# Loading w2 by two transfers (112 and 16 partitions) instead of one of 128

## The chip, the cores and the metric

The kernel runs on one core of a Trainium2 chip. The metric is the device time of one execution in microseconds (us), here the median of several runs.

## What is computed

One decode step with two branches for B = 2 tokens of width 448. Branch A is attention over the last W = 2048 positions of a key and value cache, branch B a small feed-forward net. Their product is added to the input. All inputs are bf16.

```python
xn = layernorm(x)                                  # x: 2 x 1 x 448
q = (xn @ wq).reshape(2, 1, 16, 256)               # wq: 448 x 4096
k, v = last 2048 positions of the caches           # 2 x 8 heads x 2048 x 256, each head serves 2 q heads
s = softmax(q k^T * 256**-0.5) v  -> 2 x 1 x 4096, @ wo        # wo: 4096 x 448
g = silu(relu(xn @ w1) @ w2)                       # w1: 448 x 1792, w2: 1792 x 448
out = x + s * g
```

## The kernel before

A program class, `_Prog`, keeps one list of operations for each engine. `pr.op` appends an instruction and `pr.dma` (line 34) a transfer to the list of the engine that issues it; both take a list of earlier operations to wait for. `run` turns the waits into semaphore waits: each transfer has a semaphore of its own, and each list is issued in its order. Since all operations go through this helper, all transfers carry line 35 and all matmuls line 241 in the profile, and tiles tell them apart.

**Transfers.** All large loads are issued by SP, in one queue: wq, w1, w2, then the four K tiles (`kv[0]` to `kv[3]`, 4 MB each, one for a batch and four of the eight heads), then V into the same four buffers, and last wo in six pieces (`WO_PARTS`). The first seven have nothing to wait for. V of unit u (`load_v`) waits for the last score matmul of unit u, because it overwrites K; V of unit 3 is loaded in two halves. wo overwrites wq's buffer and waits for the q matmuls. ACT's queue carries only the small loads of x and half of the output.

**w2** has 1792 x 448 elements. `w2_src` views it as 128 rows of 14 x 448 elements: partition p holds the 14 rows 14p to 14p + 13 of the matrix in one run of 12,544 bytes. `w1_sb` and `w2_sb` both appear as `w_sb` in the profile, because numbers are left out of names there.

**Order of the work.** DVE computes the layer norm; PE transposes xn and multiplies it with wq when that has landed; q is spread into a stationary form (`qstat`). Then come `do_H` (w1, relu, a transpose into `h_sb`) and `do_F`: 14 matmuls of `h_sb` with `w2_sb`, a sum over column groups, and the silu on ACT and DVE. `do_F` waits for w2, for h and for a cleared bank. After it, for each unit u, `do_turn` transposes the K tile in four pieces on DVE (line 276), `do_S` computes the scores on PE, and `do_max` and `do_et` the maximum, the exponential and its transpose. When all four units are through, `do_PV` multiplies with V unit by unit, `do_out` scales, and `do_turn_out` brings the result into the form for wo. The matmuls with wo follow as its pieces land, and two DVE instructions (lines 474 and 476) form the output. `fill` issues matmuls whose result nobody reads.

Of the kernel before, what the change touches and what calls it, by code (L numbers as in the profile page):

```python
# [11 lines left out]
PE, DVE, ACTE, SP, POOL = "pe", "dve", "act", "sp", "pool"  # L12
# [62 lines left out]
def bass_recurrent_scan__sliding_block_cached__dense_activation_relu__decode_kernel(  # L75
# [32 lines left out]
    with es:  # L108
        pr = _Prog(nc, es)

        def named(name, shape, dt):
            return es.enter_context(nc.sbuf_tensor(name, shape, dt))

        def psum(name, shape, dt):
            return es.enter_context(nc.psum_tensor(name, shape, dt))
# [48 lines left out]
        w2_sb = named("w2_sb", [128, 14 * D], BF)  # L164
# [8 lines left out]
        fbk = psum("fbk", [128, 512], F32)  # L173
# [10 lines left out]
        w2_src = B_w2.rearrange("(p j) n -> p (j n)", j=14)  # L184
# [3 lines left out]
        st = {}  # L188
        d_wq = pr.dma(SP, wqo[:, 0:SLOTS * HC], wq_src)
        st["w1"] = pr.dma(SP, w1_sb[:, :], w1_src)  # L190
        st["w2"] = pr.dma(SP, w2_sb[:, :], w2_src)
        for u in range(NU):
            d_k[u] = pr.dma(SP, kv[u][:, :], kv_src(u, A_k_cache))

# [16 lines left out]
        def z(t):  # L211
            return a_z[t.name]
# [27 lines left out]
        def mm(out_ap, lhsT, rhs, start, stop=False, **kw):  # L240
            return lambda e: e.matmul(out_ap, lhsT=lhsT, rhs=rhs, start=start, stop=stop,  # L241
                                      skip_group_check=True, **kw)
# [9 lines left out]
        deps = [d_wq, v_xr, z(qbk)]  # L252
        for s in range(SLOTS):
            for i in range(4):
# [3 lines left out]
                deps = []  # L258
# [5 lines left out]
        deps = [v_qx, st["mbk"]]  # L264
        for n in range(16):
            m_qt = pr.op(PE, mm(mbk[:, 16 * n:16 * n + 16], q_x[:, 128 * n:128 * n + 128],
                                view(ident, 0, [[32, 4], [1, 4]]), n == 0), deps)
            deps = []
# [116 lines left out]
            st["h"] = pr.op(DVE, lambda e: e.transpose(h_sb[:, :], h_n[:, :]), [v])  # L385

        def do_F():
            deps = [st["w2"], st["h"], z(fbk)]
            for j in range(14):
                i = j % 4  # L390
                o = pr.op(PE, mm(fbk[32 * i:32 * i + B, 0:D], h_sb[:, 32 * j:32 * j + 2], w2_sb[:, j * D:j * D + D],
                                 j < 4, j >= 10, tile_position=(0, 32 * i)), deps)
                deps = []
            v = pr.op(DVE, lambda e: e.tensor_copy(zc[:, :], fbk[:, 0:D]), [o])
            deps = [v, v_f8, st["mbk"]]
            for c in range(2):
                o = pr.op(PE, mm(mbk[32 * c:32 * c + B, 0:NCOL], f8[:, 0:B], zc[:, NCOL * c:NCOL * c + NCOL],
                                 True, True, tile_position=(0, 32 * c)), deps)
                deps = []
            a_e = pr.op(ACTE, lambda e: e.activation(ea[0:ROWS, :], mbk[0:ROWS, 0:NCOL], ACT.Exp, scale=-1.0), [o])  # L400
            v = pr.op(DVE, lambda e: e.tensor_scalar(
                out=ea[0:ROWS, :], in0=ea[0:ROWS, :], scalar1=1.0, scalar2=None, op0=ALU.add), [a_e])
            v = pr.op(DVE, lambda e: e.reciprocal(tmp[0:ROWS, :], ea[0:ROWS, :]), [v])
            st["g"] = st["mbk"] = pr.op(DVE, lambda e: e.tensor_tensor(
                out=g_sb[0:ROWS, :], in0=mbk[0:ROWS, 0:NCOL], in1=tmp[0:ROWS, :], op=ALU.mult), [v])
# [3 lines left out]

        do_H()  # L410
        do_F()
        do_turn(0, 0, 4)
        do_S(0)
# [31 lines left out]
        deps = [st["at"], z(wbk)]  # L445
        for j in range(WO_TILED):
# [3 lines left out]
            deps = []  # L450
# [13 lines left out]
        deps = [v_wc]  # L464
        for c in range(2):
            pr.op(PE, mm(fbk[32 * c:32 * c + B, 0:NCOL], f8[:, 0:B], wc[:, NCOL * c:NCOL * c + NCOL], False,
                         tile_position=(0, 32 * c)), deps)
            deps = []
# [42 lines left out]
```

## Time and profile before

| What | Value |
|---|---|
| median of 3 runs | 110.72 us (110.68 to 110.85) |
| the profiled execution's own time | 110.67 us |
| its span, from the first to the last instruction | 109.3 us |
| busy: PE, DVE, ACT, POOL | 57.0, 62.2, 9.1, 2.1 us |
| read from HBM | 44.11 MB, 403 GB/s over the span |
| mean granted clock of TensorE | 0.842 |

The profile is a page of one execution, and a trace that answers questions on it. Times are us from the start of the span. PE is TensorE's matmul, PEld its weight load, DVE is VectorE, ACT is ScalarE, POOL is GpSimd, SP is SyncE, and SPq is SP's issue of transfers. L35 is line 35 of the kernel. The page cuts the span into 40 equal slices (2.73 us each) and gives the busy share of each in tenths; the line DMA is the mean busy share of the core's 16 DMA engines, and GB/s is what they moved. In lists of waits and in timelines, `<-` names what released an instruction after an idle time. The chain is the sequence of work that ended last, followed back from the last instruction.

### The profile page before, as it was taken

What the parts mean: (1) busy time and instruction counts of PE and PEld (TensorE: products, weight loads), DVE (VectorE), ACT (ScalarE), POOL (GpSimd) and SP (SyncE); (2) the same over time, 40 slices, a digit from 0 to 9 for tenths busy, and PEclk for the clock granted to TensorE, in tenths of its full rate; (3) what the DMA queues carried; (4) which work ended last, traced back from release to release, by engine and by line L of the source; (5) the groups of instructions that cost most, each with busy time, mean ns of one, the idle gap of its engine ahead of it and who ended that gap; (6) DMA issues with size and microseconds to landing.
All of it is one profiled execution on the core that took longest, in us unless ns stands there. A gap on an engine that the chain in (4) does not pass through costs nothing.

```text
span 109.3 us, 1081 instructions
## 1 busy us (share of the span) xinstructions
PE 57.0 (52%) x458; PEld 14.5 (13%) x458; DVE 62.2 (57%) x83; ACT 9.1 (8%) x18; POOL 2.1 (2%) x12
## 2 busy tenths in 40 slices
PE   0010559430000079929952994499339555937791
PEld 0000114100000011001100120010023122413230
DVE  2920046445099979999999999930457333004102
ACT  3970000010000000002000200020110000000000
POOL 7000000000000000000000000000000000000000
PEclk9999999985555555999995569958995999999999
DMA  6899999999999999999999999999999899999940
GB/s 168 336 452 397 408 436 501 396 455 438 444 396 455 467 408 396 455 467 408 408 458 444 408 420 467 432 420 402 467 432 420 378 444 420 444 413 410 405 187 1
DMA packets 2616, 44.17 MB, mean 404 GB/s; under 512 B 306, under 2 KB 564, under 8 KB 948
## 3 DMA queue, kind: packets, MB, share of 16 engines
q1 hardware_dynamic: 2596, 44.11, 94.7%
q8 instruction: 3, 0.05, 0.2%
q14 instruction: 1, 0.01, 0.0%
q10 hardware_dynamic: 16, 0.00, 0.0%
HBM read 44.11 MB, written 0.00 MB: 403 GB/s over the span
## 4 chain that ended last, share of the span: by engine, by line
DMA 57%; DVE 28%; PE 7%; SPq 5%; issue 1%
DMA kv<-in_A_k_cache_dram 34%; DVE kv L276 24%; DMA wqo<-in_A_wo_dram 23%; PE sbk L241 7%; SPq L35 5%; DVE q_x L305 1%; DVE rm L293 1%; DVE rm_t L295 0%; DVE bias L299 0%; DVE bt L296 0%; DVE tmp L474 0%; DVE out_sb L476 0%; PE fbk L241 0%
## 5 line engine op out<-in xcount | busy, mean ns | idle before, releaser
L241 PE MATMUL sbk<-kv,qstat 128*8 128x512 bf16 x128 | 29.9, 1086 | 23.9 <-DVE kv L276 23.9
L276 DVE STREAM_TRANSPOSE kv<-kv 128x2048 f32<-128x2048 f32 x16 | 35.6, 2276 | 4.6 <-DMA kv<-in_A_k_cache_dram 4.6
L241 PE MATMUL obk<-kv,pt 128*16 128x512 bf16 x128 | 9.3, 435 | 4.8 <-DVE xg L356 2.4
L241 PEld LDWEIGHTS sbk<-kv,qstat 128*8 128x8 bf16 x128 | 4.0, 107 | 48.4 <-DVE kv L276 30.2
L353 DVE TENSOR_SCALAR o_odd<-obk,rs 128x256 f32<-128x256 f32 x4 | 1.9, 484 | 11.6 <-PE obk L241 11.6
L300 ACT ACTIVATE e_sb<-sbk,bias 128x512 bf16<-128x512 f32 x4 | 2.7, 687 | 52.6 <-DVE bias L299 52.6
L241 PE MATMUL qbk<-wqo,xr 128*4 128x512 bf16 x28 | 3.2, 626 | 5.7 <-DMA wqo<-in_A_wq_dram 5.7
L259 DVE TENSOR_SCALAR q_x<-qbk 128x512 bf16<-128x512 f32 x1 | 0.7, 691 | 8.7 <-PE qbk L241 8.7
L293 DVE TENSOR_REDUCE rm<-sbk 128x1 f32<-128x512 f32 x4 | 2.6, 662 | 4.7 <-PE sbk L241 4.7
L241 PE MATMUL sbk<-kv,ident 128*32 128x512 bf16 x19 | 5.1, 380 | 0.0
L241 PEld LDWEIGHTS obk<-kv,pt 128*16 128x16 bf16 x128 | 3.2, 97 | 10.1 <-issue 5.8
L305 DVE STREAM_TRANSPOSE q_x<-e_sb 128x512 bf16<-128x512 bf16 x4 | 2.8, 691 | 1.7 <-ACT e_sb L300 1.7
L241 PE MATMUL mbk<-ident,xg 2*128 2x2 bf16 x7 | 0.3, 163 | 6.0 <-DVE xg L234 6.0
L322 DVE TENSOR_TENSOR pt<-spk,pmask 128x512 bf16<-128x512 f32 x4 | 2.6, 684 | 0.7 <-PE spk L241 0.7
L241 PE MATMUL qbk<-w_sb,xr 128*2 128x448 bf16 x28 | 2.8, 572 | 0.0
L241 PE MATMUL fbk<-wqo,at 128*2 128x224 bf16 x32 | 2.5, 258 | 0.4 <-DMA wqo<-in_A_wo_dram 0.4
L241 PE MATMUL spk<-q_x,perm 128*32 128x128 bf16 x16 | 0.6, 292 | 3.1 <-DVE q_x L305 3.1
L474 DVE TENSOR_TENSOR tmp<-fbk,g_sb 34x224 f32<-34x224 f32 x1 | 0.4, 383 | 3.1 <-PE fbk L241 3.1
L270 DVE CAST qstat<-mbk 32x256 bf16<-32x256 f32 x4 | 1.7, 421 | 0.7 <-PE mbk L241 0.7
L356 DVE SCALAR_TENSOR_TENSOR xg<-obk,rs,o_odd 128x256 bf16<-128x256 f32 x4 | 1.9, 484 | 0.1
L451 DVE COPY wc<-wbk 128x448 f32<-128x448 f32 x1 | 0.6, 625 | 2.4 <-PE wbk L241 2.4
L241 PEld LDWEIGHTS sbk<-kv,ident 128*32 128x32 bf16 x19 | 1.8, 97 | 1.8
(70 smaller groups left out, 33.1 us busy)
## 6 DMA issues: line engine op xcount, KB each, us to landing
kv<-in_A_k_cache_dram SPq DMA_DIRECT2D x4, 4096.0 KB, 41.3
kv<-in_A_v_cache_dram SPq DMA_DIRECT2D x3, 4096.0 KB, 22.1
kv<-in_A_v_cache_dram SPq DMA_DIRECT2D x2, 2048.0 KB, 18.0
wqo<-in_A_wq_dram SPq DMA_DIRECT2D x1, 3584.0 KB, 11.3
w_sb<-in_B_w_dram SPq DMA_DIRECT2D x2, 1568.0 KB, 16.2
wqo<-in_A_wo_dram SPq DMA_DIRECT2D x1, 1792.0 KB, 23.7
wqo<-in_A_wo_dram SPq DMA_DIRECT2D x3, 448.0 KB, 24.8
wqo<-in_A_wo_dram SPq DMA_DIRECT2D x2, 224.0 KB, 25.5
```

The lines of the kernel that those rows point to most:

```text
L35: o = _Op(eng, lambda e: e.dma_start(dst, src), [d for d in deps if d is not None], True)
L241: return lambda e: e.matmul(out_ap, lhsT=lhsT, rhs=rhs, start=start, stop=stop, skip_group_check=True, **kw)
L259: v_q = pr.op(DVE, lambda e: e.tensor_scalar(out=view(q_x, 0, [[256, 8], [128, 2], [1, 32]]), in0=view(qbk, 0, [[64, 8], [1, 2], [2, 32]]) ...
L270: st["q"] = st["mbk"] = pr.op(DVE, lambda e, Q=Q: e.tensor_copy(qstat[32 * Q:32 * Q + 32, 256 * Q:256 * Q + 256], mbk[32 * Q:32 * Q + 32, ...
L276: st["turn", u] = pr.op(DVE, lambda e, n=n: e.transpose(kf[:, 2048 * n:2048 * n + 2048], kf[:, 2048 * n:2048 * n + 2048]), [d_k[u]])
L293: v = pr.op(DVE, lambda e: e.tensor_reduce(out=rm[:, 0:1], in_=sbk[u % 2][:, :], axis=AX.X, op=ALU.max), [last_S[u], p_z, st.get(("rmt", u ...
L300: st["exp", u] = pr.op(ACTE, lambda e: e.activation(e_sb[:, :], sbk[u % 2][:, :], ACT.Exp, bias=bias[:, 0:1], accum_out=ssum[:, u:u + 1]), ...
L305: st["et", u] = pr.op(DVE, lambda e: e.transpose(q_x[:, 512 * u:512 * u + 512], e_sb[:, :]), [st["exp", u], m_qt])
L322: st["pt", u] = pr.op(DVE, lambda e: e.tensor_tensor(out=view(pt[u], 0, [[8, 64], [2, 4], [1, 2]]), in0=view(spk, 128 * u, [[2, 64], [0, 4 ...
L353: v = pr.op(DVE, lambda e: e.tensor_scalar(out=o_odd[:, :], in0=obk[:, DH:2 * DH], scalar1=rs[:, 2 * u + 1:2 * u + 2], scalar2=None, op0=A ...
L356: st["osb", u] = pr.op(DVE, lambda e: e.scalar_tensor_tensor(out=o_sb[:, lo:lo + DH], in0=obk[:, 0:DH], scalar=rs[:, 2 * u:2 * u + 1], in1 ...
L451: v_wc = pr.op(DVE, lambda e: e.tensor_copy(wc[:, :], wbk[:, 0:D]), [o])
```

## The change

The one transfer of w2 becomes two on the same queue, one after the other: rows 0 to 111 and rows 112 to 127. Each has its own semaphore, and `do_F` waits for both. The bytes, their places and everything else stay as they were.

```diff
         st["w1"] = pr.dma(SP, w1_sb[:, :], w1_src)
-        st["w2"] = pr.dma(SP, w2_sb[:, :], w2_src)
+        st["w2a"] = pr.dma(SP, w2_sb[0:112, :], w2_src[0:112, :])
+        st["w2"] = pr.dma(SP, w2_sb[112:128, :], w2_src[112:128, :])
         for u in range(NU):
             d_k[u] = pr.dma(SP, kv[u][:, :], kv_src(u, A_k_cache))
...
         def do_F():
-            deps = [st["w2"], st["h"], z(fbk)]
+            deps = [st["w2a"], st["w2"], st["h"], z(fbk)]
```

## The prediction, made before the changed kernel ran

> **What bounds the kernel now.** I read the page's 40 slices first, then the DMA queues, the chain, and busy time by stretches.
>
> ```profile
> DMA  6899999999999999999999999999999899999940
> GB/s 168 336 452 397 408 436 501 396 455 438 444 396 455 467 408 396 455 467 408 408 458 444 408 420 467 432 420 402 467 432 420 378 444 420 444 413 410 405 187 1
> ```
> ```profile
> q1 hardware_dynamic: 2596, 44.11, 94.7%
> q8 instruction: 3, 0.05, 0.2%
> ```
>
> From the third slice to the 38th the DMA engines are busy nine tenths or more. SP's one queue (q1) carries everything but the x loads and one half of the output. The stretches give the rate (columns: start:end, length, busy us and count of PE, PEld, DVE, ACT, POOL, then PE clock, DMA share, GB/s):
>
> ```profile
> 39.00:58.00 19.00, 14.95 (x64) 1.91 (x64) 18.18 (x13) 0.78 (x2) 0.00 (x0) 0.86 1.01 437
> 58.00:77.00 19.00, 14.55 (x64) 2.04 (x64) 13.72 (x15) 1.55 (x4) 0.00 (x0) 0.74 1.01 435
> ```
>
> 436 GB/s over 16 engines is 27.25 B/ns each. At that rate the 44.11 MB of q1 need 44,110 / 436 = 101.2 us of a 109.3 us span. The trace's packet records (start, size, duration; I give their times from the span's start) agree: data runs from 1.76 us to 106.48 us, each 12,544 B packet of w2 took 469 ns, each 32,768 B packet of K and V 1,213 ns, one after another on every engine. The chain's end:
>
> ```profile
> 81.24 25.50 DMA wqo<-in_A_wo_dram
> 106.75 0.04 issue
> 106.79 0.38 PE fbk L241 x4
> 107.19 0.40 DVE tmp L474
> 107.61 0.38 DVE out_sb L476
> ```
>
> The last piece of wo waits 25 us in the queue, lands, and 1.3 us of compute and the output follow. The DVE part of the chain (24% on the K transposes) looks like a second bound, but V is issued well ahead of need: V3 at 77.5 us, while the queue still had over 8 us of V2 to move. So the end is set by the queue: what makes w2 take longer moves everything behind it by the same amount, K, the transposes, V and wo alike.
>
> **The change part by part.** *Issue on SP.* One more instruction. SP issues back to back from 0.74 us; w1 and w2 took 0.41 and 0.46 us:
>
> ```profile
> 1.20 0.92 SPq L35 DMA_DIRECT2D w_sb<-in_B_w_dram  x2
> 2.16 2.74 SPq L35 DMA_DIRECT2D kv<-in_A_k_cache_dram  x4
> ```
>
> So the four K issues move from 2.16 to about 2.6 us. K0's data starts at about 18.3 us, behind wq, w1 and w2. The cover is 16 us; cost nothing. SP's next issue, V0 at 46.54, waits for PE, not for SP.
>
> *The added wait.* PE waits for both pieces before F; the pieces' landing is what matters. What stands there now:
>
> ```profile
> L35 SPq DMA_DIRECT2D w_sb<-in_B_w_dram x2: 408/435/462, 1.2 to 1.7; - x2
> DMA to landing us min/median/max: 14.5/16.2/17.8
> ```
> ```profile
> 20.63 0.65 DVE L385 STREAM_TRANSPOSE h_sb<-h_n 128x448 bf16<-128x448 bf16 x1
> 22.34 0.62 DVE L394 COPY zc<-fbk 128x448 f32<-128x448 f32 x1 [1.06 <-PE fbk L241]
> 25.88 0.38 DVE L404 TENSOR_TENSOR g_sb<-mbk,tmp 34x224 f32<-34x224 f32 x1
> 30.05 8.89 DVE L276 STREAM_TRANSPOSE kv<-kv 128x2048 f32<-128x2048 f32 x4 [3.79 <-DMA kv<-in_A_k_cache_dram]
> ```
>
> w2 was issued at 1.66 and landed at 1.66 + 17.8 = 19.5 us; F starts at 21.38, after h (20.63 + 0.65 = 21.28). The first 1.8 us of a later landing are hidden by h. Queued behind the wait on PE is S of unit 0, and behind F's results on DVE the first K transpose; both wait for K0 anyway, with 3.79 us of idle DVE, and K0 moves with w2. Cost nothing, even if w2 is 3.8 us late.
>
> *Semaphore packets.* Every 128-row transfer ends in 16 packets of 4 B, one per engine (18 such transfers and the 2-row output give the 288 + 2 that I count on q1), of 9 ns each. One more per engine: 0.01 us.
>
> *Where the rows go.* This is the term that matters. Bytes and row size stay the same. Before, each engine took 8 rows, and sixteen streams at once did not slow one another. After, each takes 7 of the 112 rows (16 divides 112) and one of the 16 rows. If the write side of a group of eight partitions takes no more than one engine's stream (a stream never showed more than 27.25 B/ns, to eight partitions), two engines that write into one group share its rate. The trace shows no large transfer that is not 128 partitions wide, so both ends must be worked out. Lower end: streams never disturb each other, 0.01 us. The nearest row for that is x_sb: two 896 B packets to partitions 0 and 1, 1 ns apart, took 39 ns each, what 896 / 27.25 = 33 ns and some 6 ns of overhead give for one alone; but they are 14 times shorter than a w2 row. A gain is excluded here, since no engine gets less to move. Upper end: the 112 rows fill 14 groups, so 8 x 0.469 = 3.75 us where engines would need 7 x 0.469 = 3.28: 0.47 more. The last 16 rows are two groups, with sixteen engines writing: again 8 x 0.469 = 3.75 us, where alone it is 0.47: 3.28 more. Together 3.75 us.
>
> I take half, 1.9 us. The large back-to-back w2 rows resemble the second piece more than the 39 ns packets do, so it is not zero; but the engines arrive spread out (w1's semaphore packets lie between 14.54 and 15.42, 0.88 us), so that sharing is partial, an engine that is through goes on to K0, and the groups of eight may lie so that fewer than eight meet.
>
> [...]
>
> *Sum.* The profiled execution took 110.67 us (span 109.3 and 1.4 around it), 0.05 under the median of 110.72. 110.67 + 0.01 + 1.9 = 112.6 us. Late next: K0 by 1.9 us, and through the queue wo's last piece, at 108.6 instead of 106.75.
>
> **The rivals.** *No disturbance at all (chance 0.18).* The write side has room, or each engine keeps the same partitions: 110.67 + 0.01 = 110.7 us, no change. For it: the 39 ns pair. Against it: 27.25 B/ns is the ceiling of every stream, and all large streams of this trace are one to eight partitions, so the trace has never tested it.
>
> *Rows dealt unevenly to engines (0.07).* If an engine always takes eight rows, 112 rows go to 14 engines and the 16 rows to 2 of the same. These two then hold 16 rows of w2 instead of 8, 8 x 0.469 = 3.75 us more, and they set the end: 114.4 us. Against it: the four 2-row transfers on ACT's queue leave eight semaphore packets, two each, so the count of engines follows the rows and is not fixed at eight rows each. [...]
>
> *Rows dealt in turn (0.06).* If row p of the 112 goes to engine p mod 16, neighbours meet in one group all the time, not only at the edges. With two sharing throughout, w2 takes twice 3.75 us, 114.4; with four, 15.0 us, 122. Against it: nothing in the trace tells the order; for 128 rows any such order would show streams under full rate, and none is.
>
> *Faster (0.07).* The engines do not end together: their last packets end between 104.47 and 106.48, three of them late (106.12, 106.28, 106.48), the next at 105.50. The late ones had an instruction load (q8, 16,384 B) between their K and V rows: a 32,768 B packet with one beside it took 1.68 us or more instead of 1.213, and a 16,384 B packet of V by itself takes 0.61. One more DMA and wait move the instruction stream. If the loads then fall on engines that are early, the end comes 0.20 us earlier (one load) to 0.98 us earlier (all three); with 0.4, 110.3 us. It decides only where the w2 rows cost less than that. Against it: one instruction among 1081 hardly moves a load of 16 KB.
>
> **How the numbers follow.** The forecast has the remaining 0.62. Slower by over 0.2% (0.22 us, about what a measurement of this kernel can tell from no change) are the forecast and the two deals of rows: 0.62 + 0.07 + 0.06 = 0.75. Within 0.2%: 0.18. Faster: 0.07. The range must take in the no-change case, since the other cases leave out more than 0.2 without it, and the upper bound of the sharing: 110.5 to 114.4, which leaves out the dearer deals and most of the gain. The forecast's own range is 111.2 (the 112 rows' 0.47 alone) to 114.4 (all 3.75).
>
> **What would show it.** Right: packets of 12,544 B that take well over 469 ns, in the last row of each engine most; w2's second piece landing some 1 to 3 us after 19.5; K0's first transpose near 32 instead of 30.05; the wait for F still short; the end of wo near 108.6. GB/s would dip in the slices between 15 and 22 us alone. Wrong: all 256 packets still at 469 ns, which makes it the no-change case; or engines with 16 packets and others with 8; or delays of K0 that are not there at wo, which would mean that the queue has slack that I have not seen.

## The result, and the profile after

The changed kernel takes 114.31 us (median of four runs, 113.50 to 114.38), the kernel before 110.70 us beside it: a ratio of 1.0308, 95% interval 1.0268 to 1.0348, so by the ratio some 3.4 us slower (the medians differ by 3.6). The profiled execution took 113.50 us with a span of 112.2 us, 2.83 us over the one shown of before; it is the fastest of the four. The forecast of 112.6 us had the direction and the cause, but was too low by about 1.7 us: the result lies at the very top of the range of 110.5 to 114.4. One execution of the two halves below (lower and upper) took 123.57 us, at a granted clock of 0.747 where its others had 0.819 to 0.954, and is left out of the times and ratios here.

The page of the changed kernel, its 40 slices:

```profile
DMA  6898999999899899899999999999999999999950
GB/s 164 348 461 382 429 349 282 239 491 426 374 467 456 386 444 479 386 432 467 409 424 456 421 432 432 444 409 450 444 397 456 403 403 432 444 419 397 408 207 1
```

The DMA line is as full as before, but for three slices (from 14 to 22.4 us) the same busy engines move 349, 282 and 239 GB/s. Before, the lowest of these three was 396. Everything behind runs at the old rate again. The same in stretches of 3 us:

```profile
12.00:15.00 3.00, 3.00 (x28) 0.77 (x28) 0.00 (x0) 0.00 (x0) 0.00 (x0) 1.00 0.99 422
15.00:18.00 3.00, 1.61 (x32) 0.88 (x32) 2.08 (x4) 0.00 (x0) 0.00 (x0) 1.00 1.04 293
18.00:21.00 3.00, 1.83 (x20) 0.41 (x12) 1.94 (x5) 0.00 (x0) 0.00 (x0) 1.00 1.36 328
```

Before, these stretches had 431, 427 and 504 GB/s. (A packet is counted where it starts, so a short stretch can exceed the real rate.) From 15 to 18 us the DMA share is 1.04 at 293 GB/s, where before it was 1.00 at 427: the engines are as busy and move less. The packet records say the same directly: w1's 128 packets of 12,544 B take 469 ns each as before. Of the 128 of w2 only 8 do; in order of start, sixteen at a time, the medians from the second sixteen on are 694, 724, 734, 688, 646, 734 and 903 ns, and the longest takes 1,255. The longer times do not end with w2's own packets: the first K0 packet of each engine takes 1,388 to 2,752 ns, where before all sixteen took 1,213. Over these full-rate lengths, w2's packets cost each engine 1.98 us and the first K0 packet 0.95 us in the mean, together 2.93, about the 2.83 that the execution is longer.

What this does further on, first w1 (1568 KB) and w2's two pieces (the issue list, with KB and us to landing), then PE at F, then DVE:

```profile
w_sb<-in_B_w_dram SPq DMA_DIRECT2D x1, 1568.0 KB, 15.1
w_sb<-in_B_w_dram SPq DMA_DIRECT2D x1, 1372.0 KB, 20.1
w_sb<-in_B_w_dram SPq DMA_DIRECT2D x1, 196.0 KB, 20.5
```
```profile
22.70 0.92 PE L242 MATMUL fbk<-w_sb,h_sb 128*2 128x448 bf16 x14 [2.86 <-DMA w_sb<-in_B_w_dram]
```
```profile
20.54 0.65 DVE L386 STREAM_TRANSPOSE h_sb<-h_n 128x448 bf16<-128x448 bf16 x1
27.56 0.38 DVE L405 TENSOR_TENSOR g_sb<-mbk,tmp 34x224 f32<-34x224 f32 x1
33.24 8.89 DVE L277 STREAM_TRANSPOSE kv<-kv 128x2048 f32<-128x2048 f32 x4 [5.29 <-DMA kv<-in_A_k_cache_dram]
42.91 2.32 DVE L277 STREAM_TRANSPOSE kv<-kv 128x2048 f32<-128x2048 f32 x1 [0.78 <-DMA kv<-in_A_k_cache_dram]
```

PE now waits 2.86 us for w2 and starts F at 22.70 instead of 21.38. Nothing that matters waits for it: DVE is through with F at 27.94 and idle for 5.29 us before K0. K0's transposes start 3.19 us later (33.24 for 30.05) and K1's too (42.91 for 39.72). The chain's end carries it to the output, wo's last landing at 109.57 instead of 106.75:

```profile
84.47 25.10 DMA wqo<-in_A_wo_dram
109.57 0.04 issue
109.62 0.38 PE fbk L242 x4
```

### The profile page after: what moved, and what is told of

Read it like the earlier page. It is cut to its first block, busy times and chain, and to the rows that moved or that the text cites. A ratio compares the mean times of both kernels' runs of the same rounds, so it can differ in the third digit from the quotient of the medians.

```text
span 112.2 us, 1083 instructions
## 1 busy us (share of the span) xinstructions
PE 57.5 (51%) x458; PEld 15.0 (13%) x458; DVE 62.2 (55%) x83; ACT 9.1 (8%) x18; POOL 2.1 (2%) x12
## 4 chain that ended last, share of the span: by engine, by line
DMA 58%; DVE 27%; PE 7%; SPq 5%; issue 1%
DMA kv<-in_A_k_cache_dram 35%; DVE kv L277 24%; DMA wqo<-in_A_wo_dram 22%; PE sbk L242 7%; SPq L35 5%; DVE q_x L306 1%; DVE rm L294 1%; DVE rm_t L296 0%; DVE bias L300 0%; DVE tmp L475 0%; DVE bt L297 0%; DVE out_sb L477 0%; PE fbk L242 0%
## 5 line engine op out<-in xcount | busy, mean ns | idle before, releaser
L242 PE MATMUL fbk<-w_sb,h_sb 128*2 128x448 bf16 x14 | 0.9, 351 | 2.9 <-DMA w_sb<-in_B_w_dram 2.9
```

## The experiments

"Sharing" is the theory of the prediction: engines that write into the same few partitions share one write path. Its rivals: a second transfer costs by itself (issue, semaphore, a gap in the queue), or the uneven or small pieces do. In the windows quoted below the last number is GB/s. These are the same windows of the kernel before:

```profile
15.00:19.00 4.00, 2.61 (x44) 1.20 (x44) 2.93 (x6) 0.00 (x0) 0.00 (x0) 1.00 1.13 485
19.00:23.00 4.00, 1.84 (x26) 0.41 (x18) 1.89 (x3) 0.00 (x0) 0.00 (x0) 1.00 0.95 410
```

**A second transfer without other partitions.**

```diff
-        st["w2"] = pr.dma(SP, w2_sb[:, :], w2_src)
+        st["w2a"] = pr.dma(SP, w2_sb[:, 0:12 * D], w2_src[:, 0:12 * D])
+        st["w2"] = pr.dma(SP, w2_sb[:, 12 * D:14 * D], w2_src[:, 12 * D:14 * D])
```

> w2 as two transfers of 128 partitions each, split by columns (12/14 and 2/14 of each row): the second transfer, its semaphore, issue and wait stay, the partition ranges go. Sharing theory (engines that write into the same few partitions share one write path): no cost but eight more packets and a semaphore packet per engine at some 8 to 9 ns each, +0.07 us, 110.8 us, all w2 packets at their full-rate length. Rival, the second transfer as such costs the time (its issue, semaphore or a gap in the queue): 113.5 to 114.4 us as in the changed kernel.

Measured: 110.75 us, ratio 1.0005 (0.9988 to 1.0023). The packets keep their full-rate lengths (10,752 B in 404 ns, 1,792 B in 74). The issue, the semaphore, the wait and the small second transfer cost nothing that can be measured. The rival falls.

**The 16-row piece by itself**, beside an untouched w2:

```diff
         st["w2"] = pr.dma(SP, w2_sb[:, :], w2_src)
+        st["w2x"] = pr.dma(SP, kv[3][112:128, 0:14 * D], w2_src[112:128, :])
...
-            d_k[u] = pr.dma(SP, kv[u][:, :], kv_src(u, A_k_cache))
+            d_k[u] = pr.dma(SP, kv[u][:, :], kv_src(u, A_k_cache), [st["w2x"]] if u == 3 else [])
...
-            deps = [st["w2"], st["h"], z(fbk)]
+            deps = [st["w2"], st["w2x"], st["h"], z(fbk)]
```

The issue of K3 now waits for the extra load. It is through by 21.9 us, while the queue still holds K0 to K2.

> The kernel before, with an extra load of w2's rows 112 to 127 into 16 partitions (112 to 127) of the K3 buffer, which K3 overwrites later; it measures the 16-row piece by itself. Its bytes at full rate are worth 0.47 us. Without sharing: 111.2 us. Sharing in groups of eight neighbouring partitions (two groups for 16 rows): 3.75 us for the piece, 114.4 us. [...] The rival that any second transfer costs about 3 us: 113.7 us or more, and the same in the run with spread partitions.

Measured: 112.68 us against 110.75, ratio 1.0179 (1.0146 to 1.0213): 1.93 us, about four times the 0.469 us of one packet (1.88), as if the sixteen rows lay in four groups of four that take one row at a time (an estimate from these two numbers). That is 1.46 us over its bytes. Twelve packets of 12,544 B that start between 18.5 and 19.5 us take 575 to 1,441 ns, the rest of them there 469, and each engine's first K0 packet takes 1,299 to 2,427.

```profile
19.00:23.00 4.00, 1.79 (x26) 0.35 (x18) 1.83 (x3) 0.00 (x0) 0.00 (x0) 1.00 0.93 339
```

Most of the dip lies between 19 and 21 us: 187 GB/s there, where the kernel before has 426.

**The 112-row piece by itself**, in the same way (`kv[3][0:112, 0:14 * D]` from `w2_src[0:112, :]`).

> The kernel before, with an extra load of w2's rows 0 to 111 into partitions 0 to 111 of the K3 buffer; it measures the 112-row piece by itself. Its bytes at full rate are worth 7 x 0.469 = 3.28 us, so 114.0 us without sharing. Sharing, with the groups of partitions as the limit: 8 x 0.469 = 3.75 us, 114.5 us. If most of the changed kernel's cost (2.8 us) comes from this piece, it is 116 us or more.

Measured: 116.30 us, ratio 1.0505 (1.0468 to 1.0541): 5.55 us, 2.27 over its bytes. That is over both figures worked out for it. The window shows it while this piece runs:

```profile
19.00:23.00 4.00, 0.00 (x0) 0.00 (x0) 0.99 (x2) 0.00 (x0) 0.00 (x0) 0.83 1.04 294
```

The two excesses, 1.46 and 2.27, make 3.73 us; the change itself costs 3.4 (2.97 to 3.85 by the interval's ends). So the sum of the pieces agrees with the cost, and the larger part is in the large piece.

**Sixteen rows spread out** (`kv[3][0:128:8, 0:14 * D]` from `w2_src[0:128:8, :]`, the rest as above).

> As the extra 16-row load, but into partitions 0, 8, 16 ... 120 (and from the same rows of w2), one row in each group of eight neighbours. Same bytes, same number of packets, other places. Sharing in groups of eight neighbours: each engine has a group of its own, 0.47 us, 111.2 us. [...] No sharing: 111.2 us, and then the run with neighbouring partitions is 111.2 us too.

Measured: 111.98 us, ratio 1.0111 (1.0076 to 1.0145): 1.23 us, 0.76 over its bytes and 0.70 less than with neighbouring partitions. Two packets one after the other would take 2 x 0.469 = 0.94; groups of eight neighbours give 0.47. The first is nearer, and the interval (0.84 to 1.61) leaves the second out. Ten packets of 12,544 B there take 575 to 925 ns, and from 19 to 21 us 295 GB/s are moved instead of 187.

**The changed kernel once more, and in the other order.**

> The changed kernel once more beside the other splits: 113.5 to 114.4 us. Both theories expect the same; it tells how far the time moves from run to run, and so how small a difference between the splits can be read.

Measured: 114.00 us (113.59 to 114.35), ratio 1.0299 (1.0265 to 1.0332).

```diff
-        st["w2"] = pr.dma(SP, w2_sb[:, :], w2_src)
+        st["w2a"] = pr.dma(SP, w2_sb[112:128, :], w2_src[112:128, :])
+        st["w2"] = pr.dma(SP, w2_sb[0:112, :], w2_src[0:112, :])
```

> The changed kernel with the two pieces in the other order, 16 rows (112 to 127) first. Sharing theory: the same paths are shared, about the changed kernel's time, 113.5 to 114.5 us. Rival, the cost comes from the small piece standing between a large one and K0, whose rows go to the same partitions: then with the 112 rows in between part of the cost goes, 112.5 us or less.

Measured: 113.89 us, ratio 1.0306 (1.0259 to 1.0353). The order makes no difference that can be read; what lies next in the queue is not the cause.

**Two halves, lower and upper** (`0:64`, then `64:128`).

> w2 as two transfers of 64 partitions each (0 to 63, 64 to 127), four rows per engine in each. Sharing theory: 64 partitions are half of the write paths, two engines on each path all the time, so each half takes 8 x 0.469 = 3.75 us instead of 1.88, and the sum is 110.7 + 3.75 = 114.5 us, with w2's packets at about twice 0.469 us and no spread among engines beyond that. Rival, it is the uneven row count (7 and 1 per engine instead of 8) that costs: with 4 and 4 there is none, 110.8 us.

Measured: 114.95 us (median of three), ratio 1.0378 (1.0345 to 1.0411): by the ratio 4.2 us, a little over the 3.75 expected. The medians of w2's packets, sixteen at a time, run from 854 to 990 ns after the first sixteen, twice 469 and a little more. Equal row counts do not help.

```profile
15.00:19.00 4.00, 2.60 (x44) 1.18 (x44) 2.93 (x6) 0.00 (x0) 0.00 (x0) 1.00 1.03 220
```

**Two halves, even and odd** (`0:128:2`, then `1:128:2`).

> w2 as two transfers of 64 partitions each, the even and then the odd ones, four rows per engine. Both cover all write paths. If the paths belong to eight neighbouring partitions and an engine gets four consecutive rows of the transfer, each engine has its own path: 110.8 us. [...] If only the number of paths that a transfer covers counted, and not which engine writes where: 110.8 us.

Measured: 110.79 us, ratio 1.0013 (0.9995 to 1.0031). All 256 packets of w1 and w2 take 469 ns.

```profile
15.00:19.00 4.00, 2.12 (x48) 1.03 (x44) 3.05 (x7) 0.00 (x0) 0.00 (x0) 1.00 1.14 488
```

220 against 488 GB/s for the same bytes, the same four rows per engine and the same number of transfers: only the partitions differ, and with them the rows of w2 that are read. Two readings remained: paths of eight neighbours (which the 16-row runs speak against), or groups of four, as the 1.93 us suggest, with the rows dealt so that an engine stays on its own path. In the second a path has two groups of four, an estimate from the solid halves: 64 neighbours are sixteen groups, and packets of twice 469 ns are those of eight paths for sixteen engines. The next two runs tell the readings apart.

**Every fourth and every eighth partition.**

```diff
-        st["w2"] = pr.dma(SP, w2_sb[:, :], w2_src)
+        for i in range(4):
+            st["w2", i] = pr.dma(SP, w2_sb[i:128:4, :], w2_src[i:128:4, :])
```

> w2 as four transfers of 32 partitions, each taking every fourth partition (0, 4, 8 ... then 1, 5, 9 ... and so on): two rows per engine in each. If what costs is only engines meeting on one path, and a transfer's rows are dealt so that each engine gets rows from its own two groups of four (as the even and odd halves showed), then again every engine has its own path, w2's packets stay at 0.469 us, and three more semaphore packets per engine cost 0.03 us: 110.7 us. Rival, small transfers cost by themselves (four issues, four semaphores, 32 partitions): above 111.5 us.

> w2 as eight transfers of 16 partitions, each taking every eighth partition: one row per engine in each, and only one of the two groups of four neighbours is reached. [...] With paths of eight neighbours: each engine has its own, 110.8 us. By the rival that small transfers cost by themselves it is slower than with four transfers by the same amount for each transfer.

Measured: four transfers, 110.60 us, ratio 1.000 (0.998 to 1.002), all 256 packets at 469 ns. Eight transfers (the same with 8 for 4), 114.77 us, ratio 1.0382 (1.0349 to 1.0415); the medians of w2's packets run from 876 to 971 ns after the first sixteen. First the window with four, then with eight:

```profile
15.00:19.00 4.00, 2.60 (x44) 1.18 (x44) 2.93 (x6) 0.00 (x0) 0.00 (x0) 1.00 1.15 488
```
```profile
15.00:19.00 4.00, 2.60 (x44) 1.29 (x44) 2.94 (x6) 0.00 (x0) 0.00 (x0) 1.00 1.10 238
```

If the number of transfers cost, four would be slower than two. They are not, and eight cost 4.2 us at once, by the ratio, as the solid halves do; paths of eight neighbours had 110.8 us and fall. In multiples of the 469 ns the runs give: 16 neighbouring partitions about four (1.93 us for what one row per engine would do in 0.47), 64 neighbouring ones about two (medians of 854 to 990 ns), every eighth partition about two (876 to 971), every second and every fourth one. Groups of four neighbours, two to a path, would give these multiples. That is an estimate from them, and which two groups belong together no run tests.

One thing these runs do not separate: row p of w2 always goes to partition p, so each split also changes which rows are read together. Closeness of the rows is not it: every eighth row spans the whole of w2, as every fourth does, and is slow (114.77 us against 110.60). But that the packets wait on the write side, and not on the read side, is not shown; no run read the same rows into other partitions.

## Why the prediction was right, and where its size was not

*Issue on SP: right.* The K issues start at 2.67 us instead of 2.16 (I had 2.6), and the split by columns, with the same extra issue, costs nothing.

*The added wait: right.* w2's second piece was issued at 2.15 us and landed 20.5 us later, at 22.65, which is 3.1 us after the old 19.5. The first 1.8 us were hidden by h; F started 1.32 us later for the rest, and the idle DVE before K0 covered it.

*Semaphore packets: right.* q1 has 306 packets of 4 B instead of 290: sixteen for each piece, so the 112 rows and the 16 went to sixteen engines each, seven rows and one. Three more per engine (every fourth partition, ratio 1.000) cannot be told from none.

*No slack in the queue: right.* K0 and K1 are 3.19 us late, wo's last landing 2.82. The difference is one engine: of the other fifteen the median end of K0 is 2.87 us later (31.23 for 28.36), and the last one carries an instruction load (see the end).

*Where the rows go: the sharing right, its size wrong in both terms.* I forecast 1.9 us, half of an upper end of 3.75; it cost 3.4, nearly all of it. Of the two terms, the 16 rows had an upper end of 3.28, of which half is 1.64; they measured 1.46. The 112 rows had an upper end of 0.47; they measured 2.27. This is the step that failed: "the 112 rows fill 14 groups, so 8 x 0.469". That is the time of a path that is never idle while rows wait for it, so it bounds the piece from below and was no upper end at all; halving the sum hid that. By the estimate above, groups of four and two to a path, the missing 16 rows lie on four paths, so the 112 reach all sixteen, twelve with eight rows and four with four, and the busiest path has 8 x 0.469 as well; the number of paths would not explain the 2.27. What made most of their packets take 646 to 734 ns in the median, no run shows. The groups of eight neighbours were also wrong (every eighth partition cost 4.2 us, where they gave none); with groups of four the 16 rows' upper end would have been 4 x 0.469 - 0.469 = 1.41 us.

That the measured time still lies inside the range is in part luck. The 16 rows' upper end was 1.82 us too high and the 112 rows' 1.80 too low; the two errors cancel in the sum of 3.75, from which the range's top of 114.4 came.

*The row that misled:* two packets of 896 B side by side at 39 ns each. They write two neighbouring partitions, on one path by the same estimate, and are not slowed. Packets 14 times longer are: twelve of them took 575 to 1,441 ns for 469 beside the 16-row piece. What makes the difference no run here shows.

*The rivals.* No disturbance, and the gain by moved instruction loads, are out by the time. Uneven rows are out by the packet records: two engines with eight rows too many would end K0 3.75 us behind the others, while fifteen end it between 30.88 and 31.65 us, and the last at 32.78 with an instruction load. Rows dealt in turn had 114.4 us, nearer the result than the forecast, but do not fit the other splits: by the same estimate sixteen engines in step would write even partitions on eight paths at a time, at half rate, and they ran at full rate (all packets 469 ns). By it, the deal would have to keep each engine on its own path in the even and the fourfold splits; which engine takes which of the 112 rows the records do not tell, and it wasn't tried.

## What to carry to other kernels

In a kernel whose load queue never idles, look at which partitions a transfer covers before asking how many transfers there are: a split by columns, or by every second or fourth partition, was free here, while 112 and 16 partitions cost 3.4 us, and two solid halves or every eighth partition 4.2. Where streams are thought to share a resource, the work of the busiest one bounds the time from below, not from above; do not halve it to forecast. Here the 112 rows cost 2.27 us where that bound gave 0.47. In the profile, a stretch with a full DMA share and low GB/s was the sign (1.04 at 293), and packet lengths above those of the same size elsewhere settled it (medians of 646 to 903 ns for 469); include the first packet of the next transfer, which held a third of the loss here.

## What the runs showed of the hardware that was not expected

An instruction load of 16,384 B (q8) begins while K0 is on its way, at 25.8 us before and at 26.4 and 27.1 us in the two profiled executions of the changed kernel. An engine's K0 packets follow one another within a few ns (in the kernel before, the next starts 3 or 4 ns before the end of the last), so an engine can be followed through them. In all three executions the load begins 3 or 4 ns before the end of a K0 packet of one engine and takes 962 to 1,067 ns, and the next K0 packet of this engine takes 1,681 to 1,719 ns instead of 1,213. This engine ends K0 last: 0.8 us behind the next in the execution before, 1.1 (at 32.78 us) in that of 113.50 us, 2.0 (at 33.46 us) in that of 114.15. So one load cost the engine that carried it some 1.4 to 1.5 us, an estimate from these lengths, while the other fifteen went on.

Whether this engine's lateness moves the time from run to run is not shown, nor that the change makes the time move more: four runs of the changed kernel span 113.50 to 114.38 us and four more 113.59 to 114.35, and thirteen of the kernel before span 110.40 to 111.35 beside the first experiments and 110.39 to 110.90 beside the second.
